# Late weight tiles decoded through the scores' PSUM banks, weights staged in attention's idle buffers, two units of later chunks at once, and a new order

## The chip, the cores and the metric

The kernel runs on one core of one Trainium2 chip. The time is microseconds (us) on the device for one execution. TensorE (PE in the profile) multiplies matrices, VectorE (DVE) and ScalarE (ACT) work element by element, GpSimd (POOL) does a few elementwise steps that touch only SBUF, and SyncE (SP) issues the transfers. SBUF is the working memory; PSUM, eight banks of 2 KB per partition, takes the results of TensorE.

## The reference

Sliding-window attention with a window of 64 over 8 batches, 8 heads, 576 positions and 64 columns a head, and behind it a feed-forward layer with a rational function, all in float32:

```python
scores = scale * np.matmul(q, k.transpose(0, 1, 3, 2))
mask = (rel >= 0) & (rel < window)
attn = softmax(np.where(mask, scores, -1e9))
x = np.matmul(attn, v)                # as 4608 tokens x 512
h = x @ w_in                          # 2048 columns
P = a[0] + a[1] * h + a[2] * h**2 + a[3] * h**3
Q = 1.0 + np.abs(b[0]) * np.abs(h) + np.abs(b[1]) * h**2
out = (P / (Q + 1e-6)) @ w_out        # 4608 x 512
```

The weights w_in and w_out arrive as 64-bit numbers, which the kernel turns into pairs of float32 parts (high and low) by itself.

## The kernel before

**Tiling.** The 4608 tokens are cut into nine chunks of 512, the 2048 hidden columns into 16 tiles of 128. A step is one chunk with one tile; there are 144. The order of the steps is: chunk 0 with tiles 0 to 7, chunk 1 with tiles 0 to 7, chunk 1 with tiles 8 to 15, chunk 0 with tiles 8 to 15, and then chunks 2 to 8 with all 16 tiles each. So step 3 is the first that needs tile 3, steps 16 to 23 are the first that need tiles 8 to 15, and chunk 2 begins at step 32. Chunk 0's partial sums after its first eight tiles are sent to memory (`spill`) and fetched again later (`merge`).

**A unit of attention** (`plan_unit`) is one chunk with one pair of heads; a chunk has four. It loads q, k and v, computes the scores on TensorE (L419), masks and finds the maxima on VectorE, exponentiates on ScalarE, normalises on GpSimd (L457), transposes on TensorE (L462), copies the result (L466), multiplies with v (L472) and leaves x in a high and a low part. In chunks 0 and 1 the mask is added by TensorE itself (L411); from chunk 2 on by two VectorE instructions per unit (L425, one for each half).

**A gate** (`plan_gate`) is a step's h = x times w_in (12 matmuls, L525) and the rational function: three ScalarE steps, a GpSimd multiplication (L547), logarithm and exponential on ScalarE in place of a division, and six VectorE instructions (L540, L543, L557, L561, L565, L570). `plan_out` then multiplies the two parts of the gate with w_out (12 matmuls, L609) into two pairs of PSUM banks, o0 and o1.

**Decoding a weight half-tile** (`plan_decode`; a tile has two, one of w_in and one of w_out): load 512 KB into a staging buffer w_st, of which there are three (L290, L292); ScalarE scales the high word into a word tile w_c, of which there are two in SBUF (L296); GpSimd reduces the staged high word to its sign, in place (L300); VectorE puts the sign in (L304) and the low word's bits (L309); ScalarE writes the high part (L320) and VectorE the rest (L323). The word tile is held from L296 to L323.

**PSUM.** Eight banks: two for h and for the values (`ps_h`), two for the scores and the transposes (`ps_a`, the tile ps_s), four for o0 and o1.

**SBUF.** Tiles 0 to 7 have fixed places. Chunks 0 and 1 have their own early pools for attention, e0 and e1. When their units are over, these pools are closed and the same space takes tiles 8 to 11 and 12 to 15 (`Stage`). From chunk 2 on, q uses a w_c buffer, v a w_st buffer, and the unit's scores (`sm`) one buffer.

**The order of the work.** Every engine runs its instructions in the order in which they were issued. That order is fixed by `Plan.order`, which plays the program through once with the costs written at each `plan.add`, the number of buffers of each kind, and rules for TensorE's clock and for the SBUF port that VectorE and GpSimd share. At each turn it takes the instruction that can start first; among those that can start within 0.02 us of each other, the one with the lowest rank. Ranks are steps: a half-tile's is 1.5 before the step that needs it, and transfers are held back until TensorE is within four steps of their rank.

## Time and profile before

| | |
|---|---|
| median of 3 runs | 1009.49 us (1007.5 to 1012.7) |
| the profiled execution | 1008.06 us |
| its span, first to last instruction | 1006.1 us |
| mean granted TensorE clock | 0.983 |
| instructions | 16269 |
| transfers | 65.43 MB on SyncE's queue |

A row of a group reads: line, engine, operation, tiles out<-in, shapes, xcount, then busy us, the mean ns of one, the idle time before them and what ended it. A row of waits reads: engine, tile and line that waited <- engine, tile and line that released it: us in total, how often, the longest. A row of the timeline reads: start us, duration us, engine, line, operation, tiles, and in brackets the idle time just before it and its releaser. A row of one line's instructions has the minimum, median and maximum duration in ns.

### The profile page before, as it was taken

To read this page: it belongs to the slowest core of one execution; us is meant where nothing else is said; L and a number is where in the kernel's file an instruction comes from. 1 tells how busy PE (TensorE), PEld (TensorE's weight loads), DVE (VectorE), ACT (ScalarE), POOL (GpSimd) and SP (SyncE) were. 2 spreads that over 40 slices of the span, in tenths; PEclk is the share of its full clock that TensorE was granted. 3 is DMA by queue.
4 is the path that set the end of the run, shared out by engine and by line. 5 is a ranking of instruction groups with operands and counts; after the bars stand their busy time and mean duration, and the time that the engine had idled before them with its cause. 6 is when DMAs were issued, how large, how long until landed. Compare 5 with 4: busy or idle time off the path is not lost.

```text
span 1006.1 us, 16269 instructions
## 1 busy us (share of the span) xinstructions
PE 951.4 (95%) x6064; PEld 756.4 (75%) x6064; DVE 799.3 (79%) x1176; ACT 670.7 (67%) x1471; POOL 338.9 (34%) x227
## 2 busy tenths in 40 slices
PE   5778989778999999999999999999999999999998
PEld 4665667656887887788878887888788878888886
DVE  4689989987878878877778777777887778788785
ACT  5866666756775666766676667766776676656563
POOL 3536543534232223222223233233323322232322
PEclk9989999988999999999999999999999999999999
DMA  8143331242413201211130113011211111001001
GB/s 302 63 145 106 105 98 50 83 146 61 132 36 128 64 19 41 83 42 42 41 124 2 41 41 99 27 45 46 84 50 44 45 65 54 1 1 42 1 1 43
DMA packets 38959, 66.47 MB, mean 66 GB/s; under 512 B 5600, under 2 KB 21984, under 8 KB 38880
## 3 DMA queue, kind: packets, MB, share of 16 engines
q1 hardware_dynamic: 38880, 65.43, 20.2%
q8 instruction: 48, 0.79, 0.3%
q14 instruction: 31, 0.25, 0.1%
HBM read 54.92 MB, written 10.49 MB: 65 GB/s over the span
## 4 chain that ended last, share of the span: by engine, by line
PE 79%; DVE 12%; ACT 3%; issue 2%; POOL 1%; DMA 1%; SPq 0%; DVEq 0%; POOLq 0%; ACTq 0%
PE o L609 35%; PE h L525 34%; PE ps_x L472 4%; PE ps_s L419 3%; PE ps_s L462 3%; DVE u L561 2%; DVE w_c L309 1%; DVE gh L557 1%; DVE num L565 1%; DVE w_c L304 1%; DVE num L540 1%; DVE gl L570 1%; DVE num L543 1%; ACT pT L466 1%; POOL sm L457 1%
## 5 line engine op out<-in xcount | busy, mean ns | idle before, releaser
L547 POOL TENSOR_TENSOR u<-u,ah 128x512 f32<-128x512 f32 x144 | 209.6, 1456 | 432.9 <-ACT u L537 264.6
L609 PE MATMUL o<-wo_h,gl 128*128 128x512 f32 x576 | 237.0, 412 | 11.6 <-ACT wo_h L320 6.5
L525 PE MATMUL h<-xl,wi_h 128*128 128x512 f32 x576 | 229.4, 398 | 6.9 <-DVE num L543 5.4
L609 PE MATMUL o<-wo_l,gh 128*128 128x512 f32 x576 | 229.1, 398 | 2.7 <-DVE wo_l L323 2.7
L609 PE MATMUL o<-wo_h,gh 128*128 128x512 f32 x576 | 229.5, 398 | 0.0
L525 PE MATMUL h<-xh,wi_l 128*128 128x512 f32 x576 | 227.9, 396 | 1.0 <-DVE wi_l L323 0.7
L525 PE MATMUL h<-xh,wi_h 128*128 128x512 f32 x576 | 228.0, 396 | 0.0
L550 ACT ACTIVATE ah<-u 128x512 f32<-128x512 f32 x144 | 90.9, 633 | 130.1 <-POOL u L547 129.0
L557 DVE SCALAR_TENSOR_TENSOR gh<-num,a_sb,ah 128x512 fp32r<-128x512 f32 x144 | 110.4, 768 | 69.0 <-ACT ah L553 65.3
L531 ACT ACTIVATE ah<-h 128x512 f32<-128x512 f32 x144 | 85.6, 595 | 115.0 <-PE h L525 57.4
L609 PEld LDWEIGHTS o<-wo_h,gl 128*128 128x128 f32 x576 | 109.3, 190 | 43.1 <-ACT wo_h L320 7.8
L540 DVE TENSOR_TENSOR num<-num,h 128x512 f32<-128x512 f32 x144 | 98.5, 684 | 51.2 <-ACT num L534 49.7
L525 PEld LDWEIGHTS h<-xl,wi_h 128*128 128x128 f32 x576 | 108.6, 189 | 36.2 <-DVE num L543 7.4
L525 PEld LDWEIGHTS h<-xh,wi_l 128*128 128x128 f32 x576 | 108.8, 189 | 28.5 <-DVE wi_l L323 3.1
L457 POOL TENSOR_TENSOR sm<-sm,rs 128x1024 f32<-128x1024 f32 x36 | 70.9, 1970 | 174.7 <-DVE rs L453 78.6
L609 PEld LDWEIGHTS o<-wo_l,gh 128*128 128x128 f32 x576 | 109.7, 190 | 26.2 <-DVE wo_l L323 3.9
L609 PEld LDWEIGHTS o<-wo_h,gh 128*128 128x128 f32 x576 | 109.3, 190 | 25.5
L525 PEld LDWEIGHTS h<-xh,wi_h 128*128 128x128 f32 x576 | 108.9, 189 | 25.0
L537 ACT ACTIVATE u<-ah,b_sb 128x512 f32<-128x512 f32 x144 | 117.3, 814 | 0.0
L565 DVE SCALAR_TENSOR_TENSOR num<-num,a_sb,u 128x512 f32<-128x512 f32 x144 | 114.5, 796 | 1.7
L561 DVE SCALAR_TENSOR_TENSOR u<-u,gh 128x512 f32<-128x512 f32 x144 | 106.4, 739 | 8.5
L570 DVE TENSOR_TENSOR gl<-num,ah 128x512 fp32r<-128x512 f32 x144 | 111.3, 773 | 1.8
(49 smaller groups left out, 1108.8 us busy)
## 6 DMA issues: line engine op xcount, KB each, us to landing
out<-ob SPq DMA_DIRECT2D x36, 256.0 KB, 2.0
w_st<-w_in SPq DMA_DIRECT2D x16, 512.0 KB, 3.6
w_st<-w_out SPq DMA_DIRECT2D x16, 512.0 KB, 3.6
vt<-v SPq DMA_DIRECT2D x8, 448.0 KB, 4.8
vt<-v SPq DMA_DIRECT2D x8, 384.0 KB, 4.2
vt<-v SPq DMA_DIRECT2D x8, 320.0 KB, 3.5
q<-qT SPq DMA_DIRECT2D x8, 256.0 KB, 4.5
kt<-kT SPq DMA_DIRECT2D x8, 256.0 KB, 3.8
```

What stands on the lines that cost most here:

```text
L457: nc.gpsimd.tensor_tensor(out=sm, in0=sm, in1=u["rs"].unsqueeze(2).broadcast_to([P, NR, P]), op=ALU.mult)
L525: nc.tensor.matmul(h, w[i][:, cc, :], x[c, cc], start=n == 0, stop=n == 3 * NCC - 1)
L531: nc.scalar.activation(d["ah"], d["h"], AF.Abs)
L537: nc.scalar.activation(d["u"], d["ah"], AF.Identity, scale=b_sb[:, 1:2], bias=b_sb[:, 0:1])
L540: nc.vector.tensor_tensor(out=d["num"], in0=d["num"], in1=d["h"], op=ALU.mult)
L547: nc.gpsimd.tensor_tensor(out=d["u"], in0=d["u"], in1=d["ah"], op=ALU.mult)
L550: nc.scalar.activation(d["ah"], d["u"], AF.Ln, bias=QADD)
L557: nc.vector.scalar_tensor_tensor(out=d["gh"], in0=d["num"], scalar=a_sb[:, 0:1], in1=d["ah"], op0=ALU.add, op1=ALU.mult)
L561: nc.vector.scalar_tensor_tensor(out=d["u"], in0=d["u"], scalar=QADD, in1=d["gh"].bitcast(F32), op0=ALU.add, op1=ALU.mult)
L565: nc.vector.scalar_tensor_tensor(out=d["num"], in0=d["num"], scalar=a_sb[:, 0:1], in1=d["u"], op0=ALU.add, op1=ALU.subtract)
L570: nc.vector.tensor_tensor(out=d["gl"], in0=d["num"], in1=d["ah"], op=ALU.mult)
L609: nc.tensor.matmul(acc[t], g[:, ts], w[i], start=first and n == 0, stop=last and n == 2)
```

## The change

**Late tiles' words.** For tiles 8 to 15 (`i >= PSC`) the word tile is no longer in SBUF: w_in's half-tiles use the first bank of the scores' pair, w_out's the second. The pair is now one tile, `banks`, for the whole kernel; in the plan each bank is a buffer of its own, and scores from chunk 1 on and all transposes take both. VectorE's three decode instructions of these tiles no longer count as users of the shared port.

**Staging.** The first 24 half-tiles (tiles 0 to 11) are staged by turns in w_st, sm, w_st, pT, w_st, sm and vt, seven buffers that include those of later chunks' attention; the rest in w_st. Every third half-tile of tiles 0 to 7 has its words in the kt buffer, as a third word tile.

**Units.** The pool of later chunks' sm has two buffers, and vt has a buffer of its own. The two masking instructions become one over both halves with the plain mask, and a second over one block of 128 columns in each half where a sequence begins (chunks 2 to 7). Spilled partial sums leave from an sm buffer.

**Memory.** The mask has 5 blocks in place of 11; chunk 1's has a copy of its own in e1. The identity matrix is kept once. The late space is cut by half-tiles' parts instead of tiles, so tile 11 lies in both late pools and waits for both early ones.

**Order.** Some costs in the plan change, and its rules for TensorE's clock (slow by windows of 4.2 us, after a window that was less than half busy) and for the shared port. So the issued order is another one throughout.

```diff
-                if t - busy > 2.0:
-                    cold = t + 3.4
-                if t < cold:
-                    cost = min(1.83 * cost, cost + 0.83 * (cold - t) / 1.83)
-                last, busy = op.kind, t + cost
+                done_us, at = 0.0, t
+                while done_us < cost - 1e-6:
+                    w = int((at + 3.2) // 4.2)
+                    slow = 1.83 if load.get(w - 1, 0.0) < 2.1 else 1.0
+                    step = min((cost - done_us) * slow, (w + 1) * 4.2 - 3.2 - at + 1e-6)
+                    load[w] = load.get(w, 0.0) + step
+                    at += step
+                    done_us += step / slow
+                cost, last = at - t, op.kind
...
                 if e == "DVE" and t == port["POOL"]:
-                    cost = max(0.42, cost - 0.15)
-                port[e] = t + (cost - 0.02 if e == "DVE" else op.port)
+                    cost = 0.55
+                port[e] = t + (cost - 0.15 if e == "DVE" else op.port)
...
-    att = ctx.enter_context(tc.tile_pool(name="att", bufs=1))
+    att = ctx.enter_context(tc.tile_pool(name="att", bufs=2))
...
+    PSC = 8
+    WC = 2
+    banks = ps_a.tile([P, 2, 512], F32, name="banks")
...
-    plan = Plan({"w_st": 3, "w_c": 2, "kt": 1, "e0": 4, "e1": 2, "sme": 2, "pTe": 2, "sm": 1, "pT": 1, "ps_s": 1, "h": 2,
+    plan = Plan({"w_st": 3, "w_c": WC, "b0": 1, "b1": 1, "kt": 1, "e0": 4, "e1": 2, "sme": 2, "pTe": 2, "sm": 2, "vt": 1, "pT": 1, "h": 2,
                  "tmp": 2, "gp": 3, "o0": 1, "o1": 1}, 4.0)
...
-    late = [Stage(0, e0, range(H, H + H // 2), "left"), Stage(1, e1, range(H + H // 2, NF), "right")]
+    parts = tiles(H, NF)
+    half = len(parts) // 2 - 1
+    late = [Stage(0, e0, parts[:half], "left"), Stage(1, e1, parts[half:], "right")]
...
+    def staging(home):
+        if home == "w_st":
+            return stage.tile([P, 512, 2], U32, name="w_st", bufs=3)
+        pool = kv if home == "vt" else att
+        return pool.tile([P, 512, 2], U32, name="w_st", tag=home, bufs=2 if home == "sm" else 1)
+
+    def words(n):
+        if n % 3 == 2:
+            return kv.tile([P, 512], U32, name="w_c", tag="kt")
+        return stage.tile([P, 512], U32, name="w_c", bufs=WC)
+
+    HOMES = "w_st", "sm", "w_st", "pT", "w_st", "sm", "vt"
+    FROM = 24
+
-    def plan_decode(i, src, his, los, rank):
-        st, sc = Slot("w_st"), Slot("w_c")
+    def plan_decode(i, src, his, los, rank, z):
+        in_psum = i >= PSC
+        n = 2 * i + z
+        home = HOMES[n % len(HOMES)] if n < FROM else "w_st"
+        st, sc = Slot(home), Slot(f"b{z}" if in_psum else "kt" if n % 3 == 2 else "w_c")
...
-            c = d["c"] = stage.tile([P, 512], U32, name="w_c")
+            c = d["c"] = banks[:, z, :].bitcast(U32) if in_psum else words(n)
             nc.scalar.activation(c.bitcast(F32), d["w"].bitcast(F32)[:, :, 1], AF.Copy, scale=2.0 ** -111)
...
-        o = plan.add("DVE", 0.688, rank, put_sign, [o], [st, sc], 0.688)
-        o = plan.add("DVE", 0.688, rank, put_low, [o], [st, sc], 0.688)
+        o = plan.add("DVE", 0.688, rank, put_sign, [o], [st, sc], 0.0 if in_psum else 0.688)
+        o = plan.add("DVE", 0.688, rank, put_low, [o], [st, sc], 0.0 if in_psum else 0.688)
         o = plan.add("ACT", 0.63, rank, high, [o] + [x for l in late if i in l.tiles for x in held[l.n]], [sc])
-        return plan.add("DVE", 0.688, rank, rest, [o], [sc], 0.688)
+        return plan.add("DVE", 0.688, rank, rest, [o], [sc], 0.0 if in_psum else 0.688)
...
-            sqk, sq, svt, ssm, spT = Slot("kt"), Slot("w_c"), Slot("w_st"), Slot("sm"), Slot("pT")
-        sps, spt, spx = Slot(f"o{hp % 2}" if c == 0 else "ps_s"), Slot("ps_s"), Slot("h")
+            sqk, sq, svt, ssm, spT = Slot("kt"), Slot("w_c"), Slot("vt"), Slot("sm"), Slot("pT")
+        sps = [Slot(f"o{hp % 2}")] if c == 0 else [Slot("b0"), Slot("b1")]
+        spt, spx = [Slot("b0"), Slot("b1")], Slot("h")
...
-        def masked(z):
-            if z == 0:
-                u["sm"] = pool.tile([P, NR, P], F32, name="sm")
-            nc.vector.scalar_tensor_tensor(out=u["sm"][:, z * PR:(z + 1) * PR, :],
-                                           in0=u["ps"][:, z, 0:PR * P].rearrange("p (r c) -> p r c", c=P), scalar=SCALE,
-                                           in1=mm().bitcast(F32), op0=ALU.mult, op1=ALU.add)
+        def masked():
+            u["sm"] = pool.tile([P, NR, P], F32, name="sm")
+            nc.vector.scalar_tensor_tensor(out=u["sm"], in0=u["ps"].rearrange("p z (r c) -> p (z r) c", c=P), scalar=SCALE,
+                                           in1=plain(NR).bitcast(F32), op0=ALU.mult, op1=ALU.add)
+
+        def masked_first():
+            if u["first"] is None:
+                return
+            p = u["first"] // 2
+            nc.vector.scalar_tensor_tensor(out=u["sm"].rearrange("p (z r) c -> p z r c", z=2)[:, :, p, :],
+                                           in0=u["ps"][:, :, p * P:(p + 1) * P], scalar=SCALE,
+                                           in1=mask[:, 4 * (u["first"] % 2):4 * (u["first"] % 2) + 1, :].broadcast_to([P, 2, P]).bitcast(F32),
+                                           op0=ALU.mult, op1=ALU.add)
...
-            ob = e["ob"] = stage.tile([P, DO], F32, name="ob", tag="w_st", bufs=3)
+            if spill:
+                ob = e["ob"] = att.tile([P, DO], F32, name="ob", tag="sm")
+            else:
+                ob = e["ob"] = stage.tile([P, DO], F32, name="ob", tag="w_st", bufs=3)
```

More of the change, by code (lines that the diff above doesn't have):

```diff
@@ L75, in order @@
         port = {"DVE": 0.0, "POOL": 0.0}
-        last, cold, busy, now = "F", 0.0, 0.0, 0.0
+        last, now, load = "F", 0.0, {}
         for n, op in enumerate(self.ops):
@@ L212, in make_mask @@
         nc.vector.tensor_copy(out=mask, in_=raw[:, 0:1, :].broadcast_to([P, NM, P]))
-        for half, j in enumerate(KIND):
+        for half, j in ((0, 0), (1, 4)):
             hs = slice(half * 64, half * 64 + 64)
             nc.vector.tensor_copy(out=mask[hs, j, :], in_=raw[hs, 1, :])
+        nc.vector.tensor_copy(out=mask_1[:, 0, :], in_=mask[:, 4, :].bitcast(F32))
+        nc.vector.tensor_copy(out=mask_1[:, 1:PR, :], in_=mask[:, 1:PR, :].bitcast(F32))
+        make_identity(nc, raw[:, 4, :])
+        return raw[:, 4, :]
     a_sb = const.tile([P, 4], F32, name="a_sb")
@@ L237, in swa_rational_ffn, with weights, tiles, __init__ @@
     wi_h, wi_l, wo_h, wo_l = {}, {}, {}, {}
-    def weights(pool, tiles):
-        for i in tiles:
-            for d, n in (wi_h, "wi_h"), (wi_l, "wi_l"):
-                d[i] = pool.tile([P, NCC, P], F32R, name=f"{n}{i}")
-            for d, n in (wo_h, "wo_h"), (wo_l, "wo_l"):
-                d[i] = pool.tile([P, DO], F32R, name=f"{n}{i}")
+    def weights(pool, parts):
+        for d, n, i in parts:
+            d[i] = pool.tile([P, NCC, P] if n[1] == "i" else [P, DO], F32R, name=f"{n}{i}")
+    def tiles(i0, i1):
+        return [(d, n, i) for i in range(i0, i1)
+                for d, n in ((wi_h, "wi_h"), (wi_l, "wi_l"), (wo_h, "wo_h"), (wo_l, "wo_l"))]
     class Stage:
-        def __init__(self, n, early, tiles, side):
-            self.n, self.early, self.tiles, self.side = n, early, tiles, side
+        def __init__(self, n, early, parts, side):
+            self.n, self.early, self.parts, self.side = n, early, parts, side
+            self.tiles = {i for _, _, i in parts}
         def open(self):
@@ L256, in open @@
                 weights(ctx.enter_context(tc.tile_pool(name=f"late{self.n}", bufs=1, side=self.side, reuse_waits="tile")),
-                        self.tiles)
-    weights(const, range(H))
+                        self.parts)
+    weights(const, tiles(0, H))
     w_out_v = w_out.rearrange("(fc p) e -> p fc e", p=P)
@@ L365, in load_qk @@
             else:
-                q = u["q"] = stage.tile([P, TC, WIN], F32, name="q", tag="w_c")
+                q = u["q"] = stage.tile([P, TC, WIN], F32, name="q", tag="w_c", bufs=WC)
                 kt = u["kt"] = kv.tile([P, TC + 2, WIN], F32, name="kt")
@@ L382, in load_qk @@
                 kb += nw + 1
[L383 removed]
+            u["first"] = first
         def load_v():
@@ L388, in load_v @@
             else:
-                vt = u["vt"] = stage.tile([P, TC, P], F32, name="vt", tag="w_st", bufs=3)
+                vt = u["vt"] = kv.tile([P, TC, P], F32, name="vt")
             u["vw"] = []
@@ L407, in scores @@
             else:
-                ps = u["ps"] = ps_a.tile([P, 2, 512], F32, name="ps_s", bufs=1)
+                u["ps"] = ps = banks
             if on_pe:
+                m4 = mask_1 if c else mask[:, 0:PR, :]
                 for z in range(2):
-                    nc.tensor.matmul(ps[:, z, 0:PR * P].rearrange("p (r c) -> p r c", c=P), ident_r, mm(), start=True,
-                                     stop=False)
+                    nc.tensor.matmul(ps[:, z, 0:PR * P].rearrange("p (r c) -> p r c", c=P), ident_r, m4,
+                                     start=True, stop=False)
             for p in range(PR):
@@ L459, in transposes @@
         def transposes():
-            pt = u["pt"] = ps_a.tile([P, 2, 512], F32, name="ps_s", bufs=1)
+            u["pt"] = pt = banks
             for j in range(NR):
@@ L464, in copy_pT @@
         def copy_pT():
-            pT = u["pT"] = pool.tile([P, 2, PR * P], F32, name="pT")
+            pT = u["pT"] = pool.tile([P, 2, PR * P], F32, name="pT", bufs=2 if early else 1)
             nc.scalar.copy(out=pT, in_=u["pt"][:, :, 0:PR * P])
@@ L646, in plan_tiles @@
         for i in range(NF):
-            tile_in[i] = plan_decode(i, w_in[i], wi_h, wi_l, need[i] - 1.5)
-            tile_out[i] = plan_decode(i, w_out_v[:, i, :], wo_h, wo_l, need[i] + LAG - 1.5)
+            tile_in[i] = plan_decode(i, w_in[i], wi_h, wi_l, need[i] - 1.5, 0)
+            tile_out[i] = plan_decode(i, w_out_v[:, i, :], wo_h, wo_l, need[i] + LAG - 1.5, 1)
     free_x = {}
```

41 lines of the change are left out of this document (19 added, 22 removed).

## The prediction

> **What bounds the kernel now.** I read the page first, then the five engines by stretches of time.
>
> ```profile
> PE 951.4 (95%) x6064; PEld 756.4 (75%) x6064; DVE 799.3 (79%) x1176; ACT 670.7 (67%) x1471; POOL 338.9 (34%) x227
> ```
>
> ```profile
> core 0: us, PE busy (x) PEld busy (x) DVE busy (x) ACT busy (x) POOL busy (x), PEclk, DMA share, GB/s
> 0.00:25.00 25.00, 13.84 (x184) 10.27 (x184) 10.11 (x18) 12.83 (x55) 8.60 (x18) 0.93 0.84 302
> 25.00:75.00 50.00, 38.92 (x398) 30.43 (x399) 38.46 (x60) 37.90 (x119) 22.77 (x14) 0.86 0.34 105
> 75.00:225.00 150.00, 127.79 (x596) 96.51 (x594) 141.57 (x198) 96.79 (x171) 73.24 (x44) 0.97 0.30 96
> 225.00:250.00 25.00, 19.55 (x131) 15.83 (x132) 19.86 (x31) 17.50 (x40) 11.75 (x7) 0.89 0.26 76
> 250.00:900.00 650.00, 649.99 (x4324) 521.88 (x4323) 510.64 (x766) 446.08 (x998) 193.60 (x127) 1.00 0.17 54
> ```
>
> From 250 us to the end TensorE never stops (649.99 of 650 us), and the diff leaves the number of its matmuls as it is. So nothing that the change does to VectorE or ScalarE there can show, and the whole question is the first 250 us, where TensorE is idle for 11.2 + 11.1 + 22.2 + 5.5 = 50 us and its clock is below full (0.07 x 25 + 0.14 x 50 + 0.03 x 150 + 0.11 x 25 = 16 us of clock missing). The reader should see two stages. From 75 to 225 us VectorE is busy for 141.57 of 150 us, 94%: it is the bound there, carrying the gates, the decoding of weight tiles and the units at once. From 25 to 75 us it has 11.5 us free. The chain of waits of TensorE in the 75 to 225 us stretch says the same:
>
> ```profile
> PE o L609 <- ACT wo_h L320: 6.5, 3, 4.0
> PE o L609 <- DVE gl L570: 5.1, 3, 1.8
> PE o L609 <- DVE wo_l L323: 2.7, 4, 1.7
> PE h L525 <- DVE num L543: 2.0, 2, 1.9
> ```
>
> Decoded words (wo_h, wo_l) and gates (gl, num) are what it waits for. A microsecond of VectorE saved before 225 us, or moved into the free time before 75 us, is therefore taken as a microsecond off the end. Nothing after 250 us is.
>
> **Late tiles' words in PSUM.** For tiles 8 to 15 the word tile w_c moves to the two banks of the scores: 16 half-tiles, three VectorE instructions each (put_sign L304, put_low L309, rest L323). VectorE's groups between 118 and 250 us, where these run, columns busy and mean ns:
>
> ```profile
> L565 DVE SCALAR_TENSOR_TENSOR num<-num,a_sb,u 128x512 f32<-128x512 f32 x18 | 16.4, 912 | 0.0
> L561 DVE SCALAR_TENSOR_TENSOR u<-u,gh 128x512 f32<-128x512 f32 x18 | 14.8, 825 | 0.2
> ...
> L309 DVE SCALAR_TENSOR_TENSOR w_c<-w_st,w_c 128x512 uint32<-128x512 uint32 x17 | 14.5, 854 | 0.1
> ...
> L304 DVE SCALAR_TENSOR_TENSOR w_c<-w_c,w_st 128x512 uint32<-128x512 uint32 x16 | 11.4, 711 | 0.0
> L323 DVE SCALAR_TENSOR_TENSOR wo_l<-w_c,wo_h 128x512 fp32r<-128x512 f32 x9 | 6.9, 771 | 0.1
> L323 DVE SCALAR_TENSOR_TENSOR wi_l<-w_c,wi_h 128x512 fp32r<-128x512 f32 x8 | 5.5, 688 | 2.3 <-ACT wi_h L320 2.3
> ```
>
> Why the means differ shows in the spread (minimum, median, maximum) of an instruction with both inputs in SBUF and of one, of the same form, that takes an input from PSUM:
>
> ```profile
> L323 DVE SCALAR_TENSOR_TENSOR wi_l<-w_c,wi_h x16: 642/686/2386, 29.5 to 218.1; 128x512 fp32r<-128x512 f32 x16
> ```
>
> ```profile
> L425 DVE SCALAR_TENSOR_TENSOR sm<-ps_s,mask x56: 677/684/692, 218.8 to 866.7; 128x512 f32<-128x512 f32 x56
> ```
>
> Both take 685 ns undisturbed. The first is at times held up, to 2386 ns; the second never in 56 times, though GpSimd works beside it. I read this as the two-SBUF-input form waiting behind a GpSimd instruction. With c in PSUM, all three decode instructions have one SBUF input. Their 50 instructions above took 14.5 + 11.4 + 6.9 + 5.5 = 38.3 us; at 685 ns they are 34.3: 4.0 us saved. No row shows VectorE or ScalarE writing PSUM, so the price is bounded: 685 ns each (nearest, L425, reads PSUM), or 854 ns each (the dearest row), which is 42.7, a loss of 4.4. I take 685 and keep both ends. The Trainium skill (Perfetto Trace Analysis, section Optimizing Scalar/DVE Operations) gives VectorE about 125 ns of access overhead on PSUM against 60 on SBUF; by that, 48 instructions would cost an estimated 3.1 us more and the end would come 3 us later than I say. The trace's 684 against 686 ns does not agree for reads, and no run here shows writes.
>
> The gates' instructions are held up too. The same groups between 600 and 900 us, where no weights are decoded:
>
> ```profile
> L565 DVE SCALAR_TENSOR_TENSOR num<-num,a_sb,u 128x512 f32<-128x512 f32 x48 | 37.3, 777 | 0.7
> ...
> L561 DVE SCALAR_TENSOR_TENSOR u<-u,gh 128x512 f32<-128x512 f32 x48 | 34.4, 718 | 3.7
> ```
>
> Early they lose (912 - 777) + (825 - 718) = 242 ns a gate, 4.4 us over 18. With 48 instructions that can run beside GpSimd, the order has something to put there. I take 2.0 of the 4.4. What the planner makes of these freedoms the diff doesn't show, so here and below I take about half of what the rows allow.
>
> **Staging in attention's idle buffers.** Weight loads now wait for one of three w_st buffers. SyncE's waits ahead of w_in loads and the fourth and fifth of those loads:
>
> ```profile
> L290 SPq EVENT_SEMAPHORE  x17: 17/4705/13202, 24.3 to 193.5; - x17
> ```
>
> ```profile
> 34.91 0.33 SPq L290 DMA_DIRECT2D w_st<-w_in  x1
> ...
> 49.90 0.33 SPq L290 DMA_DIRECT2D w_st<-w_in  x1
> ```
>
> Seven buffers (three w_st, two sm, pT, vt) let four more 512 KB loads be issued behind the first ones, and a third word buffer (the kt tag) lets a third half-tile be in work. A half-tile is 3 x 0.686 = 2.06 us of VectorE. VectorE's 11.5 free microseconds between 25 and 75 us would hold five; ScalarE (37.9 of 50 us busy there) and the attention chain in front of it limit that. I take two and a half, 5.0 us, with bounds 0 and 11.5. The loads move past chunk 1's q, k and v on SyncE's queue: 2 MB at the 302 GB/s of the first row is 7 us of transfers. They are hidden as long as chunk 1's units are not the next need; if not, up to 3 us come back, which I keep in the range. Giving vt its own buffer, sending spilled partial sums from sm, and letting tile 11 wait for both early pools cost nothing: later chunks' units come 16 us apart (rows below), which leaves time for a v load between them, and chunk 1's units, which empty the pools, are over before its gates at step 8, half a phase before tile 11 is wanted.
>
> **Two units of a later chunk at once.** TensorE's waits between 210 and 256 us, where chunk 2's units start:
>
> ```profile
> PE ps_s L462 <- POOL sm L457: 3.2, 1, 3.2
> PE h L525 <- DVE num L543: 2.9, 1, 2.9
> ```
>
> A second sm lets the next unit's scores run while the first is normalised, which can cover the transposes' wait and loosen what stands behind it. I take 2.0 of 6.1. Late in the run units already cost no idle time.
>
> **What is added.** The two masking instructions of a unit (2 x 0.685) become one of 1024 columns and, in six chunks, one of 256. Their lengths follow from L425's 512 columns and a row of 8 columns:
>
> ```profile
> L452 DVE SCALAR_TENSOR_TENSOR sums<-sums,zero 128x8 f32<-128x8 f32 x36 | 6.4, 177 | 16.0 <-ACT sm L448 8.6 <-ACT sm L445 7.4
> ```
>
> That is (685 - 177) / 504 = 1.01 ns a column, so 1.20 us for 1024 columns and 0.43 for 256: a unit costs 0.26 us more. Two units fall in the tight stretch: 0.5 us. The rest is hidden by VectorE's idle 139 of 650 us. Smaller masks and the shared identity change only the first microseconds, ahead of the wait for q and k: nothing. The banks now have three users, and a unit's scores or transposes need both free: 2.0 us, with bounds 0 and the slow rival's price below.
>
> **The sum.** 4.0 + 2.0 + 5.0 + 2.0 - 0.5 - 2.0 = 10.5 us. About a fifth of TensorE's 50 idle microseconds go, and with them some of the 16 us of missing clock; I take 1.5. The profiled execution took 1008.06 us (span 1006.1), so it comes to 996. The median of the runs, 1009.49, lies 1.4 us above it: **997.5 us**. All gains at their upper ends (4.0, 4.4, 11.5, 6.1, no costs, 4 of clock) would give about 980.
>
> **Rivals.** First, slower: the shared banks starve chunk 2's units. The last half-tile's words today, and the units' scores with the first matmul of chunk 2's gates:
>
> ```profile
> 233.74 0.68 ACT L296 ACTIVATE w_c<-w_st 128x512 f32<-128x512 f32 x1 [0.47 <-PE ps_s L419]
> ```
>
> ```profile
> 246.27 0.69 DVE L323 SCALAR_TENSOR_TENSOR wo_l<-w_c,wo_h 128x512 fp32r<-128x512 f32 x1
> ```
>
> ```profile
> 216.64 0.45 PE L419 MATMUL ps_s<-kt,q 64*64 64x128 f32 x8 [1.10 <-DMA kt<-kT]
> ...
> 232.56 0.67 PE L419 MATMUL ps_s<-kt,q 64*64 64x128 f32 x16
> ...
> 288.31 0.40 PE L525 MATMUL h<-xl,wi_h 128*128 128x512 f32 x1
> ```
>
> A word holds its buffer from scale to rest, 13 us here. Whenever one bank comes free the next word can take it, while a unit must find both free, so units may not start before the last rest at 247 us. Four units of 16 us then end at 311 one by one, 23 us after chunk 2's gates begin now. With two at once, the first 16 us after 247 and the others d apart, they end at 263 + 3d: it decides from d = 8.4 us on. At d = 13 TensorE stands 14 us, against 8 us of gains kept: 1014 for the profiled execution, **1015.5** for the median. For it speaks the hold of 13 us; against it that the sixteen half-tiles are spread over 130 us, and that two units overlap. The Trainium skill (Perfetto Trace Analysis, section Matmuls) wants independent groups to rotate through PSUM banks so that emptying one overlaps the next; by that rule a third user of the same pair is on this rival's side, and no run here shows its price.
>
> Second, no change: the decode instructions cost 854 ns in PSUM (-4.4), and what is staged early is only decoded when VectorE has time, after 75 us as now (0 for 5.0). Then 2.0 + 2.0 - 2.5 - 4.4 is -3: 1011 for the profiled execution, **1012.5** for the median. For it speaks that VectorE's work up to 225 us is hardly less in all. This also holds if the new order keeps loads late.
>
> Third, the larger gain: the early stage fills VectorE's free time whole (11.5 for 5.0), and 3.5 us of clock come back for 1.5: 8.5 us more than the forecast, **989**. Against it: ScalarE is 76% busy there.
>
> **How the numbers follow.** Chances: forecast (991 to 1004) 0.62, larger gain 0.10, no change 0.17, slower 0.11. Half a per cent, 5 us, is about what a measurement here can tell; faster means below 1004.4, slower above 1014.5. So 0.72, 0.17 and 0.11. The range runs from 985, somewhat beyond the larger gain, to 1012, most of no change; it leaves out the slow rival and the edges.
>
> **What would show it.** Right: L304, L309 and L323 of tiles 8 to 15 near 685 ns with hardly any spread; weight loads four to seven issued before 30 us; VectorE's busy time between 25 and 75 us up by some 5 us; TensorE's idle time before 250 us down from 50 to about 40; steady running reached some 10 us earlier, and a chunk as long as now afterwards. Wrong: words in PSUM above 800 ns; scores of chunk 2 waiting for a wo_l or wi_l; a TensorE gap just ahead of chunk 2's first gate; gaps after 260 us.

## The result, and the profile after

The changed kernel takes 983.81 us, the median of 4 runs (982.67 to 984.68), beside 1010.01 us (1007.5 to 1012.7) for the kernel before on the same chip: ratio 0.9739, interval 0.9712 to 0.9767. It is 26 us faster, more than twice the 12 that were forecast. The profiled execution took 982.67 us, its span 980.9 us.

The page's first part after the change, and the same five stretches of time as shown of before (busy time of each engine, then the granted clock):

```profile
PE 941.2 (96%) x6064; PEld 749.8 (76%) x6064; DVE 774.2 (79%) x1174; ACT 670.1 (68%) x1471; POOL 336.9 (34%) x227
```

```profile
0.00:25.00 25.00, 13.25 (x184) 9.98 (x184) 9.32 (x20) 12.18 (x55) 8.61 (x18) 0.86 0.86 316
25.00:75.00 50.00, 38.42 (x402) 30.46 (x402) 38.19 (x65) 40.22 (x114) 28.77 (x17) 0.90 0.47 161
75.00:225.00 150.00, 141.12 (x681) 108.77 (x685) 144.11 (x222) 110.10 (x193) 75.59 (x47) 0.99 0.24 81
225.00:250.00 25.00, 25.00 (x253) 20.11 (x243) 20.84 (x32) 21.55 (x67) 8.03 (x5) 1.00 0.31 98
```

TensorE's idle time before 250 us is now 11.75 + 11.58 + 8.88 + 0 = 32.2 us in place of 49.9. Nothing of it went before 75 us; 13.3 us went between 75 and 225 and 5.5 behind. Its missing clock, reckoned as in the prediction, is 0.14 x 25 + 0.10 x 50 + 0.01 x 150 = 10 us in place of 16; this counts whole windows, idle time included, so it is an upper figure. Over the whole span TensorE is busy for 10.2 us less (941.2 in place of 951.4) and idle for 15.0 us less, which makes the 25.2 us by which the span is shorter. VectorE is as full as before between 75 and 225 us, but it gets 222 instructions done in 144.11 us (649 ns each) where 198 took 141.57 (715 ns each). Part of the reason shows in its groups in the stretch where tiles 8 to 15 are decoded (118 to 225 us, with 18 gates as in the prediction's rows of 118 to 250 us):

```profile
L605 DVE SCALAR_TENSOR_TENSOR num<-num,a_sb,u 128x512 f32<-128x512 f32 x18 | 13.5, 748 | 0.0
L597 DVE SCALAR_TENSOR_TENSOR gh<-num,a_sb,ah 128x512 fp32r<-128x512 f32 x18 | 13.4, 744 | 1.0 <-ACT ah L593 1.0
...
L610 DVE TENSOR_TENSOR gl<-num,ah 128x512 fp32r<-128x512 f32 x18 | 13.1, 725 | 0.1
L601 DVE SCALAR_TENSOR_TENSOR u<-u,gh 128x512 f32<-128x512 f32 x19 | 13.0, 683 | 0.3
...
L341 DVE SCALAR_TENSOR_TENSOR banks<-w_st,banks 128x512 uint32<-128x512 uint32 x16 | 11.0, 686 | 0.0
L336 DVE SCALAR_TENSOR_TENSOR banks<-banks,w_st 128x512 uint32<-128x512 uint32 x15 | 10.4, 695 | 2.1 <-issue 1.4 <-ACT banks L328 0.7
L355 DVE SCALAR_TENSOR_TENSOR wo_l<-banks,wo_h 128x512 fp32r<-128x512 f32 x8 | 5.5, 683 | 0.2 <-ACT banks L328 0.2
L355 DVE SCALAR_TENSOR_TENSOR wi_l<-banks,wi_h 128x512 fp32r<-128x512 f32 x8 | 5.4, 681 | 0.0
```

Decoding costs 681 to 695 ns in PSUM. And the gates' own instructions, which the change does not touch, are no longer held up: L565 (912 ns) is now L605 (748), L561 (825) is L601 (683). Two more of a gate's six are shorter; before, from the same view as the prediction's rows:

```profile
L557 DVE SCALAR_TENSOR_TENSOR gh<-num,a_sb,ah 128x512 fp32r<-128x512 f32 x18 | 14.6, 809 | 3.7 <-ACT ah L553 2.6 <-PE o L609 1.1
L570 DVE TENSOR_TENSOR gl<-num,ah 128x512 fp32r<-128x512 f32 x18 | 14.1, 785 | 0.0
```

So a gate is (912 - 748) + (825 - 683) + (809 - 744) + (785 - 725) = 431 ns shorter, 7.8 us over 18. The spread of one line (minimum, median, maximum) shows where holdups can still be:

```profile
L355 DVE SCALAR_TENSOR_TENSOR wi_l<-w_c,wi_h x8: 674/682/971, 30.9 to 98.8; 128x512 fp32r<-128x512 f32 x8
...
L355 DVE SCALAR_TENSOR_TENSOR wi_l<-banks,wi_h x8: 680/681/683, 125.8 to 196.2; 128x512 fp32r<-128x512 f32 x8
L355 DVE SCALAR_TENSOR_TENSOR wo_l<-banks,wo_h x8: 678/682/691, 144.0 to 215.6; 128x512 fp32r<-128x512 f32 x8
```

Words in SBUF (early tiles) still reach 971 ns; words in PSUM lie within 3 and 13 ns. TensorE's waits between 75 and 225 us, where ScalarE's wo_h (6.5 us) and gl (5.1 us) led before, now begin with these; of wo_h 0.3 us are left, of gl nothing:

```profile
PE o L649 <- DVE wo_l L355: 2.7, 2, 2.0
PE h L565 <- DVE wi_l L355: 2.5, 4, 1.0
PE h L565 <- DVE num L583: 1.8, 2, 1.0
PE o L649 <- ACT banks L328: 1.2, 1, 1.2
```

**A map for all that follows.** The first h matmul of step 12, 26 and 32 (every twelfth matmul of L525, now L565, in the timeline) cuts each span into four parts. Chunk 2 begins at step 32.

| kernel | to step 12 | 12 to 26 | 26 to 32 | 32 to the end | span |
|---|---|---|---|---|---|
| before | 132.6 | 105.2 | 50.5 | 717.8 | 1006.1 |
| after | 127.2 | 81.8 | 57.4 | 714.6 | 980.9 |
| e1 words in SBUF | 126.8 | 92.7 | 72.1 | 715.8 | 1007.3 |
| e2 rules only | 128.7 | 112.9 | 40.5 | 721.7 | 1003.8 |
| e3 staging in w_st | 134.1 | 80.1 | 57.3 | 714.2 | 985.7 |
| e4 one unit | 126.6 | 81.8 | 74.2 | 716.0 | 998.6 |
| e5 SBUF words, same order | 130.5 | 99.0 | 59.6 | 714.7 | 1003.8 |
| e6 SBUF words, own order | 127.5 | 90.4 | 58.1 | 716.4 | 992.3 |
| e7 PSUM words alone | 137.6 | 91.8 | 72.0 | 714.1 | 1015.5 |
| e8 old rules | 134.1 | 96.0 | 52.4 | 719.5 | 1002.0 |
| e9 old port rule | 138.5 | 81.3 | 64.4 | 712.7 | 996.9 |
| e10 old clock rule | 132.2 | 81.9 | 57.3 | 714.3 | 985.8 |
| e12 as e7, order jolted | 137.6 | 86.8 | 58.4 | 717.6 | 1000.4 |
| e17 PSUM words, two units | 135.9 | 82.0 | 64.0 | 713.7 | 995.6 |
| e18 as e4, order jolted | 128.8 | 97.1 | 46.6 | 719.2 | 991.7 |

The change gains 5.4 us up to step 12, 23.4 from 12 to 26, gives 6.9 back up to step 32 (16.5 net from 12 to 32), and 3.2 behind; that last column runs from 712.7 to 721.7 over all kernels with no pattern by part, so I leave it to the order.

How full VectorE is between steps 12 and 32, before and after (the third time of a row is VectorE's):

```profile
132.60:288.30 155.70, 136.46 (x812) 107.61 (x813) 134.90 (x197) 103.94 (x213) 63.02 (x40) 0.96 0.30 95
127.20:266.30 139.10, 134.76 (x828) 105.40 (x828) 128.45 (x200) 104.57 (x213) 63.21 (x40) 1.00 0.31 100
```

Of the 16.6 us only 6.4 are VectorE's busy time (134.90 to 128.45). The other 10.1 are its idle time, 20.8 us before and 10.7 after: it waited 9.6 us for ScalarE's num (L540 <- L534) and 5.7 for ah (L557 <- L553), and now 4.2 for ah and nothing for num. The 6.9 us given back are for the most part work that moved: before, VectorE did 6.1 us of chunk 2's units ahead of step 26 (masks 2.6, maxima 2.4, the rest 1.1); now all of it comes behind.

### The profile page after: what moved, and what is told of

Read it like the earlier page. It is cut to its first block, busy times and chain, and to the rows that moved or that the text cites. A ratio compares the mean times of both kernels' runs of the same rounds, so it can differ in the third digit from the quotient of the medians.

```text
span 980.9 us, 16270 instructions
## 1 busy us (share of the span) xinstructions
PE 941.2 (96%) x6064; PEld 749.8 (76%) x6064; DVE 774.2 (79%) x1174; ACT 670.1 (68%) x1471; POOL 336.9 (34%) x227
## 4 chain that ended last, share of the span: by engine, by line
PE 66%; DVE 13%; ACT 10%; issue 5%; POOL 3%; DMA 1%; SPq 0%; POOLq 0%; ACTq 0%; DVEq 0%
PE o L649 29%; PE h L565 28%; PE ps_x L511 3%; PE banks L451 3%; PE banks L501 2%; DVE num L605 2%; DVE gl L610 2%; POOL u L587 2%; ACT sm L484 1%; DVE num L583 1%; DVE gh L597 1%; DVE num L580 1%; ACT ah L571 1%; ACT num L574 1%; ACT sm L487 1%
## 5 line engine op out<-in xcount | busy, mean ns | idle before, releaser
L587 POOL TENSOR_TENSOR u<-u,ah 128x512 f32<-128x512 f32 x144 | 203.6, 1414 | 412.5 <-ACT u L577 285.6
L565 PE MATMUL h<-xl,wi_h 128*128 128x512 f32 x576 | 230.0, 399 | 5.7 <-DVE num L583 4.7
L565 PE MATMUL h<-xh,wi_l 128*128 128x512 f32 x576 | 228.6, 397 | 2.5 <-DVE wi_l L355 2.5
L565 PE MATMUL h<-xh,wi_h 128*128 128x512 f32 x576 | 227.7, 395 | 0.0
L649 PE MATMUL o<-wo_h,gh 128*128 128x512 f32 x576 | 227.2, 395 | 0.0
L565 PEld LDWEIGHTS h<-xl,wi_h 128*128 128x128 f32 x576 | 108.6, 189 | 36.5 <-DVE num L583 6.7
L496 POOL TENSOR_TENSOR sm<-sm,rs 128x1024 f32<-128x1024 f32 x36 | 74.6, 2071 | 179.4 <-DVE rs L492 132.3
L580 DVE TENSOR_TENSOR num<-num,h 128x512 f32<-128x512 f32 x144 | 98.2, 682 | 46.6 <-ACT num L574 46.1
L565 PEld LDWEIGHTS h<-xh,wi_l 128*128 128x128 f32 x576 | 108.7, 189 | 30.1 <-DVE wi_l L355 4.2
L565 PEld LDWEIGHTS h<-xh,wi_h 128*128 128x128 f32 x576 | 108.8, 189 | 24.9
L574 ACT ACTIVATE num<-h,a_sb 128x512 f32<-128x512 f32 x144 | 111.5, 775 | 0.0
L601 DVE SCALAR_TENSOR_TENSOR u<-u,gh 128x512 f32<-128x512 f32 x144 | 103.1, 716 | 8.6 <-DVE gh L597 1.8
L583 DVE SCALAR_TENSOR_TENSOR num<-num,a_sb,h 128x512 f32<-128x512 f32 x144 | 107.0, 743 | 2.7
```

The costliest lines, as they stand in the source:

```text
L496: nc.gpsimd.tensor_tensor(out=sm, in0=sm, in1=u["rs"].unsqueeze(2).broadcast_to([P, NR, P]), op=ALU.mult)
L565: nc.tensor.matmul(h, w[i][:, cc, :], x[c, cc], start=n == 0, stop=n == 3 * NCC - 1)
L574: nc.scalar.activation(d["num"], d["h"], AF.Identity, scale=a_sb[:, 3:4], bias=a_sb[:, 2:3])
L580: nc.vector.tensor_tensor(out=d["num"], in0=d["num"], in1=d["h"], op=ALU.mult)
L583: nc.vector.scalar_tensor_tensor(out=d["num"], in0=d["num"], scalar=a_sb[:, 1:2], in1=d["h"], op0=ALU.add, op1=ALU.mult)
L587: nc.gpsimd.tensor_tensor(out=d["u"], in0=d["u"], in1=d["ah"], op=ALU.mult)
```

## The experiments

The theory: words in PSUM take VectorE's decode instructions off what it shares with GpSimd, which speeds the decode itself, the gates and the steps 12 to 26. The rivals: the second unit, the early staging, or the plan's new rules carry the gain and the words' place does little. All times are medians of three rounds, ratios against the kernel before on the same chip.

### The words back in SBUF: e1, e5, e6

e1 sends all words to SBUF tiles and lets the plan find its order:

```diff
-    PSC = 8
+    PSC = 99
```

> The changed kernel with the words of all tiles in SBUF again (w_c, every third in kt); all else, the plan's new rules too, as changed. Theory A (the port): words in PSUM let VectorE decode beside GpSimd, which frees the gates too; most of the gain after step 12 goes, so 997 to 1003 us, and L605 and L601 in the late decoding stretch rise from 748 and 683 ns to 850 and more. Theory B (the order): the plan's new rules line the two engines up wherever the words lie; then 984 to 990 us and the gates' means stay below 760 ns.

Measured 1010.01 us, 0.9999 (0.9983 to 1.0015): the whole gain is gone, more than Theory A expected, while the gates' L605 and L601 rise less than it expected, from 748 and 683 to 846 and 745 ns. So not all of the loss speaks of the words' place. The late words now take turns with chunk 2's q (a w_c buffer) and k (kt), and the part from 26 to 32 pays for it, 72.1 us in place of 57.4. Its longest wait between 75 and 330 us:

```profile
PE banks L501 <- POOL sm L496: 9.4, 1, 9.4
```

So e5 puts the late words into a buffer that is idle then, vt, still reserves the banks in the plan, and tells the plan the old prices. Every engine's order is that of the changed kernel, but for three transfers on SyncE's queue (and one half-tile staged in w_st in place of vt). Only the place of the words differs.

```diff
-            c = d["c"] = banks[:, z, :].bitcast(U32) if in_psum else words(n)
+            if in_psum and "tile" not in own:
+                own["tile"] = kv.tile([P, 2, 512], U32, name="own", tag="vt")
+            c = d["c"] = own["tile"][:, z, :] if in_psum else words(n)
```

> The changed kernel with the late tiles' words in SBUF again, in the two halves of the idle vt buffer, and with the banks still reserved for them in the plan and the plan still told that they use no port. The order of every engine's instructions is that of the changed kernel (three rows of SyncE's queue apart), so only the place of the words differs. Theory A (the port frees VectorE): VectorE and GpSimd hold each other up in an order not made for it, at least the 4.0 us of decode and the gates' 7.8 us come back: 994 to 1004 us, with decode instructions at 780 ns and more. Theory C (the place does not matter, only that words no longer compete with q and k for w_c and kt): 983 to 986 us.

Measured 1005.23 us, 0.9945 (0.9926 to 0.9965): 21.4 us above the change and a little above Theory A's range; 17.2 of them lie between steps 12 and 26, where the words lie elsewhere. (3.3 lie before step 12, of these 1.8 at the first step already, long before the first late word; the 3.3 are not counted for the place.) VectorE's and GpSimd's decode groups between 118 and 225 us in e5, and GpSimd's in the changed kernel:

```profile
L339 DVE SCALAR_TENSOR_TENSOR own<-own,w_st 128x512 uint32<-128x512 uint32 x13 | 19.5, 1502 | 6.1 <-POOL w_st L335 6.0
...
L358 DVE SCALAR_TENSOR_TENSOR wi_l<-own,wi_h 128x512 fp32r<-128x512 f32 x8 | 6.1, 764 | 0.2 <-ACT wi_h L355 0.2
```

```profile
L335 POOL TENSOR_SCALAR w_st<-w_st 128x512 f32<-128x512 f32 x14 | 36.0, 2573 | 31.0 <-DVE gl L616 26.7 <-issue 2.6 <-DMA w_st<-w_out 1.4
```

```profile
L332 POOL TENSOR_SCALAR w_st<-w_st 128x512 f32<-128x512 f32 x15 | 27.2, 1816 | 25.4 <-DVE gl L610 21.2 <-DVE num L605 2.0 <-ACT banks L328 1.6
```

put_sign (L339) goes from 695 to 1502 ns with the same order and the same data, and GpSimd's own step from 1816 to 2573: each holds the other up. The Trainium skill (SBUF — State Buffer, section Who interferes with whom) says that VectorE contends with a GpSimd instruction that reads SBUF if both of its inputs lie in SBUF, and not if at most one does. The trace agrees: 1502 against 695 ns. TensorE then waits for the gates, in e5 between 75 and 330 us:

```profile
PE h L571 <- ACT ah L599: 9.0, 6, 1.9
PE h L571 <- DVE num L589: 8.6, 6, 3.1
```

e6 is e5 with the plan told what such words cost, so that it can keep them apart from GpSimd:

```diff
-        o = plan.add("DVE", 0.688, rank, put_sign, [o], [st, sc] + sv, 0.0 if in_psum else 0.688)
+        o = plan.add("DVE", 0.688, rank, put_sign, [o], [st, sc] + sv, 0.688)
```

(put_low and rest likewise.)

> As the run before, with the plan told that these words use the shared port, so that it can make an order for that. Theory A: part of the loss is planned away, 990 to 1000 us. Theory C: 983 to 987 us. If it is above the run before, the plan's port rule itself is at fault.

Measured 995.42 us, 0.9859 (0.9839 to 0.9878), 11.6 us above the change. put_sign is back at 681 ns, but the holdups sit in the gates again, as before the change:

```profile
L611 DVE SCALAR_TENSOR_TENSOR num<-num,a_sb,u 128x512 f32<-128x512 f32 x17 | 15.7, 926 | 0.0
L607 DVE SCALAR_TENSOR_TENSOR u<-u,gh 128x512 f32<-128x512 f32 x17 | 13.1, 773 | 0.6
```

The order that avoids them on put_sign moves them to the gates; with the words in PSUM they are on neither. That the place does it is shown by e5, where next to nothing else differs. With an order of its own the place is worth 11.6 us, to within what the orders themselves do (below): e6 is one order, and lies 3.2 us above the slowest order of the changed kernel. Between steps 12 and 32 of e6:

```profile
127.50:275.90 148.40, 137.43 (x825) 108.67 (x825) 134.55 (x199) 107.17 (x228) 65.33 (x41) 0.95 0.31 100
```

With all changed but the place, VectorE is as busy as before (134.55 us, 134.90 before), and its idle time falls from 20.8 to 13.9 us. The place then takes the busy time to 128.45 and the idle time to 10.7.

### The parts one by one: e2, e3, e4, e7, e17

e2 is the kernel before with the new rules of the plan and its three changed costs (the diff's hunks of Plan.order; 2.78, 0.695 and 1.9 us), nothing else.

> The kernel before with only the plan's new rules for TensorE's clock and for the shared port, and its three changed costs: no new buffers, no PSUM words. Theory A: the order alone gives little, 1003 to 1011 us. Theory B: the order gives most of it, 985 to 996 us.

Measured 1005.71 us, 0.9962 (0.9944 to 0.9981). The rules alone give 4 us, and step 12 comes 3.9 us earlier by them.

e3 is the changed kernel with everything staged in w_st:

```diff
-    FROM = 24
+    FROM = 0
```

> The changed kernel with all weights staged in the three w_st buffers (the third word tile stays). Theory A gives early staging about 5 us, the lead at step 12: 987 to 991 us. Rival: what is late early is caught up, since VectorE is the bound until 215 us anyway and its work does not grow: 984 to 985.5 us. Rival: staging is half the gain: 994 us or more.

Measured 988.83 us, 0.98 (0.9775 to 0.9824): 5.0 us above the change. Step 12 comes 6.9 us later and the parts behind it are the same to 1.7 us, so what this order loses, it loses before step 12, where staging was expected to gain.

e4 keeps two sm buffers but allows one later unit at a time: a new pool "one", held from a unit's scores to its transposes.

```diff
+        one = [] if early else [Slot("one")]
...
-... scores, [o, chain.get("scores")], [sqk, sq, ssm] + sps, kind="S"))
+... scores, [o, chain.get("scores")], [sqk, sq, ssm] + sps + one, kind="S"))
...
-... transposes, [o, chain.get("transposes")], [ssm] + spt, kind="T"))
+... transposes, [o, chain.get("transposes")], [ssm] + spt + one, kind="T"))
```

> The changed kernel with one unit of a later chunk at a time: a unit holds a single token from its scores to its transposes; the second sm stays for staging. Theory A gives the overlap 2 to 4 us, all of it before chunk 3: 986 to 988 us. Rival: units of later chunks do not matter: 983 to 985 us. Rival: with the banks shared, units that start late cannot catch up one by one: 992 us or more, with a gap ahead of step 32.

Measured 1001.2 us, 0.9919 (0.9897 to 0.9941). Up to step 26 it is the changed kernel to 0.6 us; then chunk 2's units come too late. TensorE stands before step 32, in the window and the waits between 225 and 305 us:

```profile
250.00:300.00 50.00, 37.72 (x349) 29.32 (x346) 27.19 (x44) 23.74 (x70) 9.44 (x6) 0.86 0.30 93
```

```profile
PE o L650 <- DVE gl L611: 4.8, 1, 4.8
PE banks L502 <- POOL sm L497: 4.7, 3, 3.0
```

e7 is the other way round: the kernel before with the late words in the banks (b0, b1) and nothing else, without staging, rules or second unit.

```diff
-        st, sc = Slot("w_st"), Slot("w_c")
+        in_psum = i >= 8
+        st, sc = Slot("w_st"), Slot(f"b{z}" if in_psum else "w_c")
```

> The kernel before with only the late tiles' words moved to the scores' banks; one unit at a time, staging and the plan's rules as before. Theory A by my sum: 4 us of decode and up to 7.8 us of the gates, less what late units cost: 998 to 1006 us. Theory D (the parts need each other): shared banks make chunk 2's units late, and one at a time they give it all back as in the run with one unit, 1003 to 1014 us, with a TensorE gap ahead of step 32.

Measured 1017.33 us, 1.0066 (1.0044 to 1.0089): slower than before, and above both ranges that were expected. This is the prediction's slow rival. The part from step 12 to 26 is 13.4 us shorter (here too chunk 2's units come behind it), and the part from 26 to 32 is 21.5 longer, with one unit at a time: step 32 comes at 301.4 us in place of 288.3. The stretch and its longest wait:

```profile
250.00:300.00 50.00, 38.21 (x368) 30.96 (x370) 30.74 (x48) 26.32 (x74) 10.30 (x7) 0.90 0.34 107
```

```profile
PE banks L465 <- POOL sm L460: 9.1, 1, 9.1
```

e17 adds the second unit to that, and with it v's own buffer and the small edits of mask and costs: the changed kernel with the old rules, staging in w_st and no words in kt.

> The changed kernel with the plan's old rules, staging in w_st alone and no third word tile: of the change there remain words in PSUM, two units at once, v's own buffer and the small edits of mask and costs. The old rules cost 20 us and w_st staging 5 on the changed kernel, each alone. If the parts just add: 1008 us. If PSUM words and the second unit are the core and the rest mostly finds an order: 995 to 1004 us.

Measured 995.81 us, 0.9858 (0.9831 to 0.9884). Words, second unit and these small edits together give 14.5 us, 9.7 of them between steps 12 and 32 (146.0 us in place of 155.7).

### The rules of the plan: e8, e9, e10

The changed kernel with both old rules (e8), with the old rule for the port alone (e9, below), and with the old one for the clock alone (e10, the diff's first hunk turned round).

```diff
-                    cost = 0.55
-                port[e] = t + (cost - 0.15 if e == "DVE" else op.port)
+                    cost = max(0.42, cost - 0.15)
+                port[e] = t + (cost - 0.02 if e == "DVE" else op.port)
```

> The changed kernel with the old rules of the plan for TensorE's clock and the port (the new costs stay). Alone on the kernel before the new rules gave 0.4%, about 4.5 us. Theory A: about the same here, 985 to 990 us. Theory B (the order is what counts): 995 us or more. If words in PSUM leave the port rule little to do: 983 to 985 us.

> The changed kernel with only the plan's port rule put back (what a VectorE instruction costs that waits for GpSimd, and how long it holds the port); the new clock rule stays. The old rules together cost 20 us on the changed kernel. If the port rule carries it (GpSimd and VectorE are lined up wrongly, gates held up again): 998 to 1004 us. If the clock rule carries it: 983 to 988 us. In between if both do.

> The changed kernel with only the plan's rule for TensorE's clock put back. If the plan's picture of the slow clock in the first 100 us carries the 20 us: 996 to 1004 us. If the port rule does: 983 to 988 us.

Measured 1003.71 us (0.9942, 0.9921 to 0.9963), 998.79 (0.9908, 0.9883 to 0.9934) and 987.96 (0.9797, 0.9772 to 0.9822). On top of the other parts the new rule for the port is worth 15 to 16 us (e9 against the change, e8 against e10), that for the clock 4 to 5, though both together give 4 alone (e2). These are single orders, though: e17 has both old rules and no early staging besides, and is 8 us faster than e8. In e8 some of the gates' instructions are held up again: between 118 and 225 us L606 (gl) takes 782 ns and L593 (gh) 809, where the changed kernel has 725 and 744. But that is not the old rules' doing alone. In e17, with the same old rules, L606 and L593 take 724 and 744 ns, and the two lines that the prediction priced are those of the changed kernel too (748 and 683 there):

```profile
L601 DVE SCALAR_TENSOR_TENSOR num<-num,a_sb,u 128x512 f32<-128x512 f32 x18 | 13.5, 749 | 0.1
L597 DVE SCALAR_TENSOR_TENSOR u<-u,gh 128x512 f32<-128x512 f32 x18 | 12.3, 681 | 0.1
```

So words in PSUM can free the gates without the new rules. (In e7, with the old rules too, one of the four, L568, still takes 886 ns.) Summed over its six VectorE instructions, a gate of steps 12 to 25 takes 4.33 to 4.47 us in the thirteen kernels with words in PSUM and 4.47 to 4.71 in the seven without. What the port rule does show is ahead of step 12, where the words lie in SBUF in every kernel: the first 48 VectorE instructions of decoding take 798 to 859 ns on average in the eight kernels with the old port rule and 708 to 789 in the twelve with the new one. In e9 it is 802 ns against the change's 746, so 2.7 us of its 15. How much of the rest is the rule and how much the order is not separated.

### How much an order is worth by chance: e11 to e16, e12, e18

The order is built greedily, so a change of any price reshuffles all of it. The changed kernel and the kernel before, each with one number changed that means nothing: the gate's cost by 0.01 us, or the 0.02 us within which ranks decide.

```diff
-        f = f1[s] = plan.add("PE", 2.78, s, products, x_ready[c] + [tile_in[i], f1.get(s - 1)], [sh])
+        f = f1[s] = plan.add("PE", 2.77, s, products, x_ready[c] + [tile_in[i], f1.get(s - 1)], [sh])
```

> The changed kernel with one cost in the plan, a gate's 12 matmuls, at 2.77 in place of 2.78 us: no edit to the work, only another order. Theory L (the order's luck): a list order that takes what can start first lands far away after the smallest change, and part of the differences of the runs before is that: 988 us or more. If the order is robust: 982 to 987 us.

> The changed kernel with ties of 0.03 in place of 0.02 us in the plan's order. Theory L (luck is part of it): 985 to 994 us. If the run with 2.77 was the exception: 982 to 985 us.

> The changed kernel with a gate's cost in the plan at 2.79 us. Theory L: 985 to 994 us. If the run with 2.77 was the exception: 982 to 985 us.

> The kernel before with ties of 0.03 in place of 0.02 us in the plan's order. If the port bounds it whatever the order: 1006 to 1012 us. Theory L for both kernels: as far as 1000 or 1018 us.

> The kernel before with a gate's cost in the plan at 2.77 in place of 2.76 us. If the port bounds it whatever the order: 1006 to 1012 us. Theory L for both kernels: as far as 1000 or 1018 us.

| kernel | number | us | ratio (interval) |
|---|---|---|---|
| after | as it is: 2.78, tie 0.02 | 983.81 | 0.9739 (0.9712 to 0.9767) |
| e14, after | 2.79 | 984.01 | 0.9748 (0.973 to 0.9767) |
| e13, after | tie 0.03 | 985.73 | 0.9768 (0.9748 to 0.9789) |
| e11, after | 2.77 | 992.2 | 0.984 (0.982 to 0.986) |
| e16, before | 2.77 for 2.76 | 1010.93 | 1.0014 (0.9997 to 1.0031) |
| e15, before | tie 0.03 | 1014.02 | 1.005 (1.0032 to 1.0068) |

The two families do not overlap: four orders of the changed kernel have a mean of 986.4 us, three of the one before 1011.7. The gain of 25 us is the change's. But 0.01 us in one price can move 8 us, so a difference of 4 to 8 us between single orders (e2, e3, e10) is not evidence by itself. The two verdicts that rest on a gap ahead of step 32 got a second order each, tie 0.05 for e7 and 0.0 for e4:

> The kernel with PSUM words alone (1017 us) with one number of the plan's order changed: instructions that can start within 0.05 in place of 0.02 us of each other go by rank. Theory D (shared banks starve chunk 2's units when they come one at a time, whatever the order): 1012 to 1020 us with a gap ahead of step 32. Theory L (that gap is one order's outcome): 996 to 1004 us, with chunk 2's first unit before the last word, and that is what PSUM words are worth alone.

> The run with one unit at a time (1001 us) with a tie width of 0 in place of 0.02 us in the plan's order. If one unit at a time cannot catch up behind the shared banks: 997 to 1004 us again, with a TensorE gap ahead of step 32. If it was that order's luck: 985 to 993 us.

e12: 1003.31 us, 0.9935 (0.99 to 0.997); e18: 993.62 us, 0.9838 (0.9814 to 0.9863). Neither has the gap (e18's TensorE stands 2.7 us between 250 and 300 us); e12 there:

```profile
250.00:300.00 50.00, 50.00 (x412) 40.43 (x405) 39.49 (x61) 35.72 (x92) 14.29 (x10) 1.00 0.25 80
```

So the missing second unit costs 17 us in one order (e4) and 10 in the other (e18), and words in PSUM alone are 7 us slower than before in one and 6 faster in the other. The smaller differences put the second unit at some 8 to 10 us (e17 against e12, which differ in the small edits too, and the change against e18). That is hardly more than one order moves, and e18 lies only 1.4 us above e11. A sign that does not hang on one order, though its ranges overlap, is VectorE's idle time between steps 12 and 32: 15.9 to 30.7 us in the eight kernels with one unit at a time, 9.8 to 19.7 in eleven of the twelve with two (e1, whose words take q's and k's buffers, has 31.8). The rest of the two gaps was those orders' luck.

## Why the prediction was right and wrong

**Right:** the sign, the stretch, and that words in PSUM free the decode and the gates. Little was to be won behind chunk 2's start: from step 32 to the end 3.2 us went, and chunks 3 to 8 are as long as before to about 2 us. All of the gain that a part can be named for lies ahead of step 32. That a microsecond of VectorE saved is a microsecond off the end was only half of it: between steps 12 and 32 more went of VectorE's waiting than of its work (10.1 and 6.4 us).

**Decode in PSUM, 4.0 us:** as predicted; 685 ns was taken, 681 to 695 measured. The second rival's 854 ns is refuted. The Trainium skill's larger overhead on PSUM (Perfetto Trace Analysis, section Optimizing Scalar/DVE Operations) would make it an estimated 65 ns more each. The trace does not agree: with its input in PSUM L355 has a median of 681 ns against 682 for the early tiles; with input and output in PSUM L336 has 698 against 684 and L341 685 against 686, so 14 ns more at most.

**Early staging, 5.0 us:** the number is right by luck (5.0 by e3, one order; 5.4 by the lead at step 12), and the working is wrong. Weight loads do move forward: with one at 12.30 us, eight are issued before 25 us, where it was four. On SyncE's queue:

```profile
17.27 1.65 SPq L322 DMA_DIRECT2D w_st<-w_in  x2
...
19.91 0.43 SPq L324 DMA_DIRECT2D w_st<-w_out  x1
20.39 1.41 SPq L322 DMA_DIRECT2D w_st<-w_in  x1
21.84 0.43 SPq L324 DMA_DIRECT2D w_st<-w_out  x1
22.48 0.33 SPq L322 DMA_DIRECT2D w_st<-w_in  x1
24.48 11.13 SPq L324 DMA_DIRECT2D w_st<-w_out  x2
```

Yet VectorE's busy time between 25 and 75 us is not up by 5, it is 38.19 us in place of 38.46. It does five instructions more in the same busy time. The free time that the term was sized by is still free: up to step 12 VectorE's idle time rises from 28.3 to 29.8 us, and its busy time falls from 104.3 to 97.4. What got shorter is the early decode, whose words still lie in SBUF: its 48 instructions take 746 ns on average in place of 859, which is 5.4 us. The rules have at least as much part in that as the staging: alone they give 789 ns and 3.9 us of the lead (e2), while early staging with the old port rule gives 802 ns and no lead (e9; it reaches step 12 at 138.5 us, before at 132.6).

**The first step that failed: the gates' holdups, "I take 2.0 of the 4.4".** Two things were wrong with it. The upper end was too low: it priced L565 and L561 alone and took their means late in the run (777 and 718 ns) as undisturbed. They take 748 and 683 now, so those means held holdups of their own, and L557 and L570 gain as well: 7.8 us over 18 gates. The kernel before had the price: over its whole run the four lines have medians of 747, 693, 751 and 691 ns, and the means of 118 to 250 us lie 165 + 132 + 58 + 94 = 449 ns above them, 8.1 us over 18 gates. And "about half of what the rows allow", because the diff doesn't show what the planner makes of its freedoms, went the wrong way. It did not take a better planner: e17, with the old rules, has the gates of the changed kernel.

**The second, and larger: the waits, "2.0 of 6.1" for the second unit less 2.0 for the banks.** The sum put the waits of the stretch at nothing, while VectorE's idle time between steps 12 and 32 fell by 10.1 us, 6.9 of them with the words still in SBUF (e6). VectorE's own terms there, 4.0 + 2.0 - 0.5 = 5.5, stand against 6.4 us of busy time: in total they were nearly right, as gates and decode take 8.7 us less there and the units 2.3 more. The two terms are also not independent. Without the second unit the change is 10 to 17 us slower (e4, e18). How much of the 10.1 us is the second unit and how much the order is open. The slow rival was real: it is e7, and e4 has its gap. In the changed kernel it did not come. Chunk 2's scores there:

```profile
218.71 1.10 PE L451 MATMUL banks<-kt,q 64*64 64x128 f32 x32
224.69 1.10 PE L451 MATMUL banks<-kt,q 64*64 64x128 f32 x32
...
241.43 1.10 PE L451 MATMUL banks<-kt,q 64*64 64x128 f32 x32
246.84 1.10 PE L451 MATMUL banks<-kt,q 64*64 64x128 f32 x32
```

The rival's condition held: the first scores start at 218.71 us, behind the last word, which left the banks at 216 us (the last rest of wo_l from banks starts at 215.6). But the rival reckoned with 247 there, and the units' scores come in pairs, 6 us apart. It missed that the words which hold the banks are themselves done 30 us sooner.

**Clock, 1.5 of 16 us:** by the same reckoning 6 came back. The granted clock rose where TensorE's idle time went (0.97 to 0.99 between 75 and 225 us, 0.89 to 1.00 from there to 250) and fell in the first 25 us, from 0.93 to 0.86.

**Masking, +0.5 us:** 1.22 and 0.41 us were measured for the estimates of 1.20 and 0.43, over the whole run:

```profile
L456 DVE SCALAR_TENSOR_TENSOR sm<-banks,mask 128x1024 f32<-128x1024 f32 x28 | 34.2, 1222 | 29.0 <-PE banks L451 29.0
...
L463 DVE SCALAR_TENSOR_TENSOR sm<-banks,mask 128x256 f32<-128x256 f32 x24 | 9.9, 414 | 0.0
```

**The form of the sum** failed as well. Taken away one by one, the parts cost 5 (staging), 12 to 21 (place), 10 to 17 (second unit) and 20 (rules): far more than 26 together. Alone, the rules give 4 us, and words in PSUM give 6 or cost 7. They need one another. From step 12 to 32 the sum had 4.0 + 2.0 + 2.0 - 0.5 - 2.0 = 5.5 us, and 16.5 were measured; that is 11.0 of the 13.2 us by which the forecast fell short (12 forecast, 25.2 measured on the span).

**Open:** of the 15 to 20 us of the rules (e8, e9) some 3 are the early decode; how much of the rest is their better picture of the port and how much the luck of those orders is not known, as they were run with one order each. And why TensorE still stands 23 us before 75 us, as before.

## What to carry to other kernels

Where VectorE is the bound and GpSimd works beside it, look at the spread of each two-input form: a long upper tail with a clean median (here 686 ns, with a maximum of 2386) can be a holdup by the neighbour. The mean less the median prices it, for the instructions around as well as for those you would move; putting one operand in idle PSUM took it off both here. Before you credit a shorter stretch to the engine that bounds it, split it into that engine's busy and idle time. When a buffer gets another user, ask who must now wait for the whole of it, and give that one a second place to go on. Where the order comes from a greedy plan, run an ablation under two orders before you believe a difference of a few microseconds.

## What the hardware showed that was not expected

GpSimd loses about as much as VectorE where the two meet: its sign step rose from 1816 to 2573 ns in e5, put_sign from 695 to 1502. And ScalarE writes PSUM faster than SBUF, 636 against 684 ns for the same scaling (in e5, where the late words lie in SBUF, their median is 671):

```profile
L328 ACT ACTIVATE w_c<-w_st 128x512 f32<-128x512 f32 x16 | 10.6, 684 | 2.1 <-issue 1.4 <-DVE wo_l L355 0.5 <-DVE wi_l L355 0.2
L328 ACT ACTIVATE banks<-w_st 128x512 f32<-128x512 f32 x16 | 10.2, 636 | 5.3 <-DVE wo_l L355 2.8 <-DVE wi_l L355 2.5
```
